# Two weight loads asked for by another engine, and four gates computed in one go, in a fused attention and mixture-of-experts kernel

## The chip, the cores and the metric

The kernel runs on one core of a Trainium2 chip. The time is device microseconds from launch to end, lower is better, given as the median of several executions. The profile shows one more execution, in which every instruction was recorded; its "span" runs from the first instruction to the last.

A core has five engines that run side by side, each through its own list of instructions in order: PE (TensorE, matrix products), DVE (VectorE), ACT (ScalarE), POOL (GpSimd) and SP (SyncE, which here only asks for transfers). Transfers between the main memory and the on-chip memory (DMAs) are asked for by SP, ACT or POOL, each through a queue of its own, and carried out by 16 DMA engines[...]. [...]

## What is computed

```python
def reference(**kwargs):
    attn_out = _attn_ref(q, k, v)            # softmax attention inside chunks of 64 tokens
    x = attn_out.transpose(0, 2, 1, 3).reshape(B * S, H * D)      # 4608 tokens x 512
    return _moe_ref(x, expert_emb, tau, w1, w2)

def _moe_ref(x, expert_emb, tau, w1, w2):
    ...
    logits = xn @ en.T / tau                 # 8 experts
    expert_idx = np.argmax(logits, axis=1)
    probs = softmax(logits)
    gate_w = probs[np.arange(N), expert_idx]
    for e in range(E):
        mask = expert_idx == e
        h = np.maximum(x[mask] @ w1[e], 0.0)               # 512 -> 1024
        out[mask] = gate_w[mask, None] * (h @ w2[e])       # 1024 -> 512
    return out
```

All of it is in 32-bit floats. Each token goes to the one expert that fits it best, and its output is scaled by the gate, the softmax weight of that expert. Since the chosen expert has the largest logit, the gate is 1 / sum(exp((logit - max) / |x|)).

## The kernel before

**Two stages.** The first, some 170 us, computes attention for 36 blocks of 128 tokens, finds each token's expert, and writes each token's row (512 values, its 8 logits, its number and its sum of squares) with an indirect DMA from POOL into `spots`, a table in main memory that is sorted by expert. The second stage runs over *steps*. A step takes two groups of 64 tokens, one from each of two streams: stream s = 0 works upwards from expert 0, stream s = 1 downwards from expert 7. The first four steps (NE = 4) are sure to belong to experts 0 and 7; for the later ones DVE works out tables (`src_row`, `eblk`, `fresh`, `swap`, `after`, `more_e`) in `places` and `behind`, at the turn from the first stage to the second.

**What a step j does.** SP loads the tokens' rows with `load_x(j)`: for each stream two DMAs into `xin` (three buffers) and one small one into `spot`. DVE turns the rows (`turn_xb`) and adds up quarters of them (`add_x`). `gate_parts(j)` computes the gate: a square root on ACT, four small instructions on DVE, an exponential with a sum on ACT, two small instructions on DVE. It is a generator, so its caller places each piece among other work. `hidden_fast(j)` computes relu(x @ w1) by Strassen's scheme in Winograd's form: seven products p1, p2, p3, p5, p6, p7, p4, in this order, of quarters of x with quarters of w1 (B11, B12, B21, B22) and with their differences T1, T2, T3, T4. PE does the products (L337), ACT copies the first out of PSUM (the tile U) and applies the relu, DVE combines (L369). `result(j)` multiplies by w2 (64 records on L408), ACT scales with the gate into `y`, of which there is one buffer, and POOL writes the rows to the output by an indirect DMA (L427). In the loop, pass j does hidden_fast(j + 1) and then result(j).

**The differences of w1.** `add_up(s, ...)` has DVE compute T1 to T4, 128x1024 values each (L286). For the first experts, T1, T2 and T4 of stream 0 come in pass 0 and of stream 1 in pass 1; T3 replaces B12 itself, and so comes in pass 1 after step 2, which still uses plain products (`hidden_plain`). T3 is first used by p7 of hidden_fast(3).

**Weights.** w1 and w2 of one expert are 2 MB each, per stream, so a load of both streams is 4 MB. `w2_sb` has two buffers, alternating from step 5 on (LONE = 5): the steps 0 to 4 use buffer 0. `load_when` asks for a load under a condition that is read from a table: `fresh` is 0 where a buffer holds the right expert already, and then nothing moves, but PE's wait on the load still ends only when SP has come to it. For step 5 the condition always holds, as buffer 1 is empty. `next_w1` holds w1 of the expert to come; `load_behind(j)` asks for it under the condition `more_e`, which is always true for the first one, j = 3. `take_next(j)` takes it over at a change of expert: three copies on POOL and the differences on DVE. In the trace the first such copy is at 298 us.

**SP's order around the change.** SP works through its list strictly in order: load_x(4), load_x(5), load_w2(5); pass 1: load_x(6), load_behind(3); pass 2: load_x(7), load_behind(4); pass 3: load_x(8), load_w2(4), load_behind(5); pass 4: load_x(9), load_w2(6), and so on. The order was written by hand (`manual_schedule`); the waits between engines come from the tile framework. POOL's list there: the last rows and padding rows into `spots`, a memset of `pad_late`, then one output DMA per step, and the copies of take_next.

**Pads.** `pad` sets a few unused floats at the start of a memory pool, which shifts the addresses of what follows. The pools `keep` and `blk` lie below all others; `qk` (first stage) and `late` (second stage) begin at the same place above them.

Of the kernel before, what the change touches and what calls it, by code (L numbers as in the profile page):

```python
# [9 lines left out]
FP32 = mybir.dt.float32  # L10
BF16 = mybir.dt.bfloat16
I32 = mybir.dt.int32
AF = mybir.ActivationFunctionType
ALU = mybir.AluOpType
# [4 lines left out]
P = 128  # L19
# [6 lines left out]
def kernel(  # L26
# [36 lines left out]
    def buf_of(j):  # L63
        return 0 if j < LONE else (j - LONE + 1) % 2
# [66 lines left out]
    def number(ap, top, *engines):  # L131
        return nc.values_load(  # L132
            ap,
            engines=engines,
            min_val=0,
            max_val=top,
            skip_runtime_bounds_check_because="a count of comparisons, less than this",
        )
# [27 lines left out]
        r0 = (0, E - 1)[s] * R + G * j  # L166
        return spots[r0 : r0 + G * n, :]

    def load_when(w, rows, e, f):

        e, f = number(e, E - 1, ENG.SP), number(f, 1, ENG.SP)
        nc.sync.dma_start(
            out=whole(w), in_=rows[:, ds(e, 1), :], cond=f > 0, max_dma_last_dim=4096
        )

    def load_w2(j):
        for s in range(2):
            at = of_step(s, j)
            load_when(w2_sb[s][buf_of(j)], w2_rows, eblk[at], fresh[at])

    def load_behind(j):

        c = LEAST - 2 - j
        for s in range(2):
            at = (slice(G * s, G * s + 1), slice(c, c + 1))
            load_when(next_w1[s], w1_rows, after[at], more_e[at])

    def load_late(j):
        for s in range(2 if j != LEAST else 1):
# [21 lines left out]

    def gate_parts(j):
        lg = spot[:, j % SPOTS, 0:E]
        rn = bp.tile([P, 1], FP32, tag="rn", name="rn", bufs=4)
        lmax = bp.tile([P, 1], FP32, tag="lmax", name="lmax", bufs=4)
        sh = bp.tile([P, E], FP32, tag="sh", name="sh", bufs=4)
        last = "_last" if j == LEAST - 1 else ""
        gate = bp.tile([P, 1], FP32, tag="gate" + last, name="gate", bufs=5)
        nc.scalar.activation(rn, spot[:, j % SPOTS, SQ : SQ + 1], AF.Sqrt)  # L219
        yield  # L220
        nc.vector.tensor_reduce(lmax, lg, axis=AX.X, op=ALU.max)
        nc.vector.tensor_scalar(rn, rn, 1e-6, None, ALU.add)  # L222
        nc.vector.reciprocal(rn, rn)
        nc.vector.tensor_scalar(sh, lg, lmax, rn, ALU.subtract, ALU.mult)
        yield
        nc.scalar.activation(sh, sh, AF.Exp, accum_out=gate)  # L226
        yield
        nc.vector.tensor_scalar(gate, gate, 1e-9, None, ALU.add)
        nc.vector.reciprocal(gate, gate)
        gate_of[j] = gate  # L230

    def hidden_part(j, s, b, w1, pool, tag, ps=None):

# [211 lines left out]
    with (  # L445
# [13 lines left out]
        NX = 2 * RB  # L459
        xr = one.tile([P, NX, W], FP32, name="xr")  # L460
        blank = one.tile([P, W], FP32, name="blank")
        pad(qk_p, 40, "pad_qk")
        ident = one.tile([P, P], FP32, name="ident")
        make_identity(nc, ident)
        rl_ps = ps_l.tile([P, 4 * RB * E + 2 * P], FP32, name="rt_ps")
# [638 lines left out]
        places(0, 2)  # L1104
        turn_xb(2)
        early_parts(NT + 3, 0)
        first_gates = [gate_parts(j) for j in range(4)]
        for g in first_gates:
            next(g)
        places(2, NST)  # L1110
        nc.vector.tensor_copy(n_steps, mid[0:1])
        nc.vector.tensor_copy(n_odd, odd[0:1])
        behind()

    late_p = ctx.enter_context(tc.tile_pool(name="late", bufs=1, reuse_waits="tile"))
    pad(late_p, 40, "pad_late")
    for s in range(2):
        w2_sb[s].append(late_p.tile([P, KF, D], FP32, name=f"w2_{s}1"))

# [2 lines left out]

    load_x(NE)
    load_x(NE + 1)
    load_w2(LONE)

    with (
        tc.tile_pool(name="ps_h", bufs=1, space=PSUM, reuse_waits="tile") as ps_h,
        tc.tile_pool(name="ps_y", bufs=2, space=PSUM, reuse_waits="tile") as ps_y,
    ):  # L1130
        H_PS = [P, G // Q, KF * Q]

        def hidden_plain(j, w1, behind_it=None):
            for s in range(2 if j != LEAST else 1):
                ps = bank(ps_h, H_PS)
                for b in range(G // Q):
                    hidden_part(j, s, b, w1, None, None, ps)
                if behind_it is not None:
                    behind_it(s)

        def first_parts():
            for g in first_gates:
                next(g, None)

        first_parts()
        for j in range(LEAST - 1):
            n = j + 2

            def turn_next():
                if n < LEAST:  # L1150
                    turn_xb(n)
                    if n + XBUF < NJ:
                        load_x(n + XBUF)
                    add_x(n)

            def swap_next():
                if NE <= n < LEAST:
                    take_next(n)

            if j == 0:  # L1160
                first_parts()
                add_up(0, None, TS)
                first_parts()
            elif j == 1:
                turn_next()
                add_up(1, None, TS)
                hidden_plain(2, w1_sb, lambda s: add_up(s, None, ("T3",)))
            else:
                gate = gate_parts(n) if n < LEAST else iter(())
                hidden_fast(j + 1, ps_h, gate, turn_next, swap_next)  # L1170

            result(j, ps_y)
            if NE <= next_of(j) < NJ:
                load_w2(next_of(j))
            if NE - 1 <= n < LEAST - 1:
                load_behind(n)
            elif n == LEAST - 1:
                load_late(LEAST)

        steps = number(n_steps, NST, ENG.PE, ENG.DVE, ENG.Activation, ENG.Pool, ENG.SP)  # L1180

        odd_one = number(n_odd, 1, ENG.PE, ENG.DVE, ENG.Activation, ENG.Pool, ENG.SP)

        def before_last():
            result(LEAST - 1, ps_y)
            load_w2(LEAST + 1)

        def step_alone(j, between=None):
            turn_xb(j)
            if j + XBUF < NJ:  # L1190
                load_x(j + XBUF)
            gates(j)
            hidden_plain(j, next_w1)
            if j + 1 < NJ:
                load_late(j + 1)
            if between is not None:
                between()
            result(j, ps_y)
            if j + 2 < NJ:
                load_w2(j + 2)  # L1200

        def more(j):
            if j == NJ:
                return

            with tc.If(steps > j - NE - 1):  # L1206
                step_alone(j)
                more(j + 1)

        had, had_mo, had_gate = dict(xin), dict(mo), dict(gate_of)  # L1210
        with tc.If(odd_one > 0) as if_odd:  # L1211
            step_alone(LEAST, before_last)
            more(LEAST + 1)
        for now, then in ((xin, had), (mo, had_mo), (gate_of, had_gate)):
            now.clear()
            now.update(then)
        with if_odd.Else():
            del xin[LEAST]
            load_x(LEAST + XBUF)
            before_last()  # L1220
            load_w2(LEAST + 2)
            load_late(LEAST + 1)
            more(LEAST + 1)
# [28 lines left out]
```

## Time and profile before

| | |
|---|---|
| median of 3 runs | 657.39 us (654.38 to 658.06) |
| the profiled execution | 657.75 us, span 656.0 us |
| PE busy | 617.0 us, 94% of the span |
| ACT busy | 429.7 us, 66% |
| DVE busy | 425.3 us, 65% |
| POOL busy | 183.9 us, 28% |
| DMA queue q1 (SP's): moved, share of the 16 engines' span | 71.99 MB, 34.0% |
| DMA queue q0 (POOL's) | 38.89 MB, 17.5% |
| PE's granted clock, mean | 0.993 |

A line of the timeline has the start in us, the length in us, the engine, the line of the code, the operation, its output and inputs, and the number of instructions merged into it; in brackets stands how long the engine sat idle before it and what ended that. "SPq" is SP's queue: what is listed there is the issue of a DMA, not its transfer. A line of waits has the waiting instruction, what it waited for, and then the total in us, how often, and the longest.

### The profile page before, as it was taken

The page shows a single profiled execution, that of the slowest core. Times are in us where ns is not written, and L with a number is a line of the kernel's source. Part 1 is how long each engine was busy: PE and PEld are TensorE (multiplying, and loading weights), DVE is VectorE, ACT ScalarE, POOL GpSimd, SP SyncE. Part 2 cuts the span into 40 slices and gives each one's busy share as a digit, 9 for nine tenths or more (in the row PEclk, how much of TensorE's full clock was granted, in tenths as well). Part 3 has the DMA queues.
Part 4 walks back from the last instruction along what each step waited for, and adds up shares of the span by engine and source line. Part 5 has one row for each costly group of instructions (what it writes and reads, how often), then busy time and mean ns, then how long its engine had stood idle before and what let it go on. Part 6 is the DMA issues. An engine that isn't in the chain of part 4 may idle for free. (4 is left out here: it accounts for less than half of the span.)

```text
span 656.0 us, 24867 instructions
## 1 busy us (share of the span) xinstructions
PE 617.0 (94%) x9744; PEld 344.5 (53%) x9744; DVE 425.3 (65%) x1140; ACT 429.7 (66%) x758; POOL 183.9 (28%) x262
## 2 busy tenths in 40 slices
PE   6899989898898989999999999999999999999993
PEld 5778878775443435445444544665444444444431
DVE  4878888786697446647784566979546666654430
ACT  4767767674316757767676767776777777676650
POOL 7759897762410100003020002303010021000101
PEclk9999999999998999999999999999999999999998
DMA  9999999988528711112787111776821116311111
GB/s 259 302 253 276 275 293 283 333 280 299 220 64 304 285 41 40 46 39 72 285 316 265 53 44 43 292 302 236 341 62 44 47 39 217 129 39 35 51 32 36
DMA packets 91696, 112.68 MB, mean 172 GB/s; under 512 B 49260, under 2 KB 69484, under 8 KB 91560
## 3 DMA queue, kind: packets, MB, share of 16 engines
q1 hardware_dynamic: 79512, 71.99, 34.0%
q0 software_dynamic: 12016, 38.89, 17.5%
q8 instruction: 81, 1.33, 0.8%
q14 instruction: 55, 0.45, 0.2%
q10 hardware_dynamic: 32, 0.02, 0.0%
HBM read 334.71 MB, written 22.69 MB: 545 GB/s over the span
## 5 line engine op out<-in xcount | busy, mean ns | idle before, releaser
L408 PE MATMUL y_ps<-w,hT 128*32 128x512 f32 (+1 forms) x2368 | 278.0, 587 | 2.9 <-DMA w<-in_moe_w_dram 2.9
L356 ACT ACTIVATE h<-C 64x256 f32<-64x256 f32 x264 | 179.4, 679 | 69.9 <-DVE C L369 67.1
L408 PEld LDWEIGHTS y_ps<-w,hT 128*32 128x32 f32 x2368 | 91.2, 110 | 155.4 <-issue 136.0
L427 POOL DMA_INDIRECT out_dram<-y,spot x36 | 37.5, 1042 | 392.4 <-ACT y L420 301.6
L337 PE MATMUL h<-w,S 128*32 128x256 f32 x1056 | 108.4, 382 | 1.8 <-DVE w L286 1.8
L337 PE MATMUL h<-sums,xbT 128*32 128x256 f32 x1056 | 109.0, 383 | 0.5 <-DVEq L294 0.5
L369 DVE TENSOR_TENSOR C<-C,h 128x256 f32<-128x256 f32 x231 | 96.0, 416 | 11.2 <-PE h L337 4.4
L363 DVE STREAM_TRANSPOSE hT<-h 128x512 f32<-128x512 f32 x66 | 46.7, 708 | 55.2 <-ACT h L356 54.5
L337 PE MATMUL h<-w,xbT 128*32 128x256 f32 x1056 | 82.3, 379 | 0.0
L222 DVE TENSOR_SCALAR rn<-rn 128x1 f32<-128x1 f32 x37 | 5.6, 151 | 87.6 <-ACT rn L219 87.6
L337 PEld LDWEIGHTS h<-w,S 128*32 128x32 f32 x1056 | 49.3, 110 | 24.2 <-DVE w L286 1.5
L337 PEld LDWEIGHTS h<-sums,xbT 128*32 128x32 f32 x1056 | 49.4, 111 | 23.2 <-DVEq L294 1.4
L337 PEld LDWEIGHTS h<-w,xbT 128*32 128x32 f32 x1056 | 43.6, 110 | 31.6 <-issue 9.0
L420 ACT ACTIVATE y<-y_ps,gate 128x512 f32<-128x512 f32 x36 | 24.8, 688 | 50.6 <-issue 44.7
L337 PE MATMUL h<-sums,S 128*32 128x256 f32 x528 | 53.4, 379 | 0.0
L816 POOL DMA_INDIRECT spots<-xr,dest x36 | 37.4, 1039 | 28.0 <-DVE dest L781 9.8
L198 DVE STREAM_TRANSPOSE xbT<-xin 128x256 f32<-128x256 f32 x73 | 44.4, 646 | 0.5 <-DVE hT L363 0.5
L219 ACT ACT_TABLE_LOAD x34 | 43.6, 1283 | 0.9 <-issue 0.4
L226 ACT ACT_TABLE_LOAD x34 | 43.6, 1283 | 0.6
L698 ACT COPY xT<-tr 128x512 f32<-128x512 f32 x36 | 21.1, 586 | 32.3 <-PE tr L696 32.3
L586 POOL DMA_DIRECT2D kx<-in_k_dram x36 | 31.9, 888 | 13.4 <-PE tr L612 12.6
L586 POOL DMA_DIRECT2D qx<-in_q_dram x40 | 34.5, 865 | 0.7 <-PE tr L612 0.6
(204 smaller groups left out, 802.2 us busy)
## 6 DMA issues: line engine op xcount, KB each, us to landing
w<-in_moe_w_dram SPq DMA_DIRECT2D x74, 2048.0 KB
next_w<-in_moe_w_dram SPq DMA_DIRECT2D x67, 2048.0 KB
xin<-spots SPq DMA_DIRECT2D x158, 64.0 KB
qx<-in_q_dram POOLq DMA_DIRECT2D x32, 256.0 KB, 5.9
v<-in_v_dram SPq DMA_DIRECT2D x58, 128.0 KB
kx<-in_k_dram POOLq DMA_DIRECT2D x28, 256.0 KB, 4.6
spots<-blank SPq DMA_DIRECT2D x9, 144.0 KB
spot<-spots SPq DMA_DIRECT2D x80, 4.0 KB
```

The costliest lines, as they stand in the source:

```text
L198: nc.vector.transpose(xT[:, :, cols].rearrange("p c (b i) -> p b c i", i=Q), t[:, s * (D // 2) : (s + 1) * (D // 2)].rearrange("p (b i c) ...
L219: nc.scalar.activation(rn, spot[:, j % SPOTS, SQ : SQ + 1], AF.Sqrt)
L226: nc.scalar.activation(sh, sh, AF.Exp, accum_out=gate)
L337: nc.tensor.matmul(ps[t0 : t0 + Q], lhsT=a[:, c, s], rhs=w[:, r], start=c == 0, stop=c == KD // 2 - 1,)
L356: nc.scalar.activation(h[b][G * v : G * v + G, s].rearrange("p (k i) -> p k i", i=Q), x[G * s : G * s + G].rearrange("p (i k) -> p k i", i=Q),
L363: nc.vector.transpose(hT.rearrange("p k (s b i) -> p b s k i", b=2, i=Q)[:, b], h[b].rearrange("p s (k i) -> p s k i", i=Q),)
L369: nc.vector.tensor_tensor(out, a, b, op)
L408: nc.tensor.matmul(ps[Q * r : Q * r + Q, 0:w], lhsT=d["hT"][:, c, Q * t0 : Q * t0 + Q], rhs=w2_sb[s][buf_of(j)][:, c, d0 : d0 + w], start= ...
L420: nc.scalar.activation(y[:, 0:w], ps[:, 0:w], AF.Copy, scale=gate_of.pop(j))
L427: ins = nc.gpsimd.indirect_dma_start(out=to, out_offset=bass.IndirectOffsetOnAxis(ap=at, axis=0), in_=y[:, 0:w], in_offset=None, bounds_ch ...
L586: eng.dma_start(out=x[done : done + n], in_=src[b, :, s : s + n, :].rearrange("h p d -> p h d"),)
L816: ins = nc.gpsimd.indirect_dma_start(out=spots, out_offset=bass.IndirectOffsetOnAxis(ap=at, axis=0), in_=m, in_offset=None, bounds_check=S ...
```

## The change

The change has three parts. The load of w2 for step 5 and the first load of the next w1 (load_behind(3)) are asked for by POOL instead of SP; both keep their place in the code, and thus come on POOL's list after the memset of pad_late and after the output DMA of step 1. The gates of steps 0 to 3 are computed by one set of instructions on tiles of four columns; the sum of the exponentials becomes a reduction on DVE. Some small tiles get two buffers instead of four, and two pads are 32 floats instead of 40.

```diff
-    def load_when(w, rows, e, f):
-        e, f = number(e, E - 1, ENG.SP), number(f, 1, ENG.SP)
-        nc.sync.dma_start(
+    def load_when(w, rows, e, f, by=(nc.sync, ENG.SP)):
+        e, f = number(e, E - 1, by[1]), number(f, 1, by[1])
+        by[0].dma_start(
             out=whole(w), in_=rows[:, ds(e, 1), :], cond=f > 0, max_dma_last_dim=4096
         )
+    BY_POOL = (nc.gpsimd, ENG.Pool)
-    def load_w2(j):
+    def load_w2(j, *by):
...
-    def load_behind(j):
+    def load_behind(j, *by):
...
     def gate_parts(j):
-        rn = bp.tile([P, 1], FP32, tag="rn", name="rn", bufs=4)
-        lmax = bp.tile([P, 1], FP32, tag="lmax", name="lmax", bufs=4)
-        sh = bp.tile([P, E], FP32, tag="sh", name="sh", bufs=4)
+        rn = bp.tile([P, 1], FP32, tag="rn", name="rn", bufs=2)
+        lmax = bp.tile([P, 1], FP32, tag="lmax", name="lmax", bufs=2)
+        sh = bp.tile([P, E], FP32, tag="sh", name="sh", bufs=2)
...
+    def first_gate_parts():
+        lg, sq = spot[:, 0:NE, 0:E], spot[:, 0:NE, SQ]
+        rn = bp.tile([P, NE], FP32, name="rn4", bufs=1)
+        lmax = bp.tile([P, NE], FP32, name="lmax4", bufs=1)
+        sh = bp.tile([P, NE, E], FP32, name="sh4", bufs=1)
+        gate = bp.tile([P, NE], FP32, name="gate4", bufs=1)
+        nc.scalar.activation(rn, sq, AF.Sqrt)
+        yield
+        nc.vector.tensor_reduce(lmax, lg, axis=AX.X, op=ALU.max)
+        nc.vector.tensor_scalar(rn, rn, 1e-6, None, ALU.add)
+        nc.vector.reciprocal(rn, rn)
+        for by, op in ((lmax, ALU.subtract), (rn, ALU.mult)):
+            nc.vector.tensor_tensor(sh, lg, by.unsqueeze(2).to_broadcast([P, NE, E]), op)
+            lg = sh
+        yield
+        nc.scalar.activation(sh, sh, AF.Exp)
+        yield
+        nc.vector.tensor_reduce(gate, sh, axis=AX.X, op=ALU.add)
+        nc.vector.tensor_scalar(gate, gate, 1e-9, None, ALU.add)
+        nc.vector.reciprocal(gate, gate)
+        for j in range(NE):
+            gate_of[j] = gate[:, j : j + 1]
...
-        pad(qk_p, 40, "pad_qk")
+        pad(qk_p, 32, "pad_qk")
...
-        first_gates = [gate_parts(j) for j in range(4)]
-        for g in first_gates:
-            next(g)
+        first_gates = first_gate_parts()
+        next(first_gates)
...
-    pad(late_p, 40, "pad_late")
+    pad(late_p, 32, "pad_late")
...
-    load_w2(LONE)
+    load_w2(LONE, BY_POOL)
...
-        first_parts()
+        next(first_gates)
         for j in range(LEAST - 1):
...
             if j == 0:
-                first_parts()
+                next(first_gates)
                 add_up(0, None, TS)
-                first_parts()
+                next(first_gates, None)
...
             if NE - 1 <= n < LEAST - 1:
-                load_behind(n)
+                load_behind(n, *([BY_POOL] if n == NE - 1 else []))
```

## The prediction

> **What bounds the kernel now.** I read the page's busy table first, then who TensorE waited for, then the timeline around those waits. PE is busy 617.0 of 656.0 us. From 175 us on it is the bound: its result() blocks repeat every 12.92 us (last three lines of the PE fence below: 236.02, 248.96, 261.87) and it hardly stops. So this change can only win where PE stops between 178 and 240 us, the steps it touches.
>
> PE's waits between 178 and 240 us (total, times, longest): there are two reasons only, one for each half of the change.
> ```profile
> PE y_ps L408 <- DMA w<-in_moe_w_dram: 2.9, 2, 2.6
> PE h L337 <- DVE w L286: 1.8, 2, 1.0
> ```
> PE's timeline (start, length): products of hidden_fast(3), then result() of steps 4, 5 and 6.
> ```profile
> 199.16 1.05 PE L337 MATMUL h<-sums,S 128*32 128x256 f32 x16
> 201.00 0.63 PE L337 MATMUL h<-w,S 128*32 128x256 f32 x4 [0.80 <-DVE w L286]
> 202.66 1.44 PE L337 MATMUL h<-w,S 128*32 128x256 f32 x10 [1.03 <-DVE w L286]
> ...
> 234.71 1.05 PE L408 MATMUL y_ps<-w,hT 128*32 128x512 f32 x4 [2.63 <-DMA w<-in_moe_w_dram]
> ...
> 236.02 6.63 PE L408 MATMUL y_ps<-w,hT 128*32 128x512 f32 x58 [0.26 <-DMA w<-in_moe_w_dram]
> ...
> 248.96 6.61 PE L408 MATMUL y_ps<-w,hT 128*32 128x512 f32 x58
> 261.87 6.61 PE L408 MATMUL y_ps<-w,hT 128*32 128x512 f32 x58
> ```
> *Stop A* (200.2 to 202.7): product p7 wants T3 of both streams from DVE. DVE's timeline shows why T3 is late: it works without a gap from 185.5 on, and the gates stand in front.
> ```profile
> 185.59 0.15 DVE L221 TENSOR_REDUCE lmax<-spot 128x1 f32<-128x8 f32 x1
> ...
> 188.19 1.22 DVE L286 TENSOR_TENSOR sums<-w 128x1024 f32<-128x1024 f32 x1
> ...
> 191.84 0.15 DVE L228 TENSOR_SCALAR gate<-gate 128x1 f32<-128x1 f32 x1
> ...
> 192.88 1.23 DVE L198 STREAM_TRANSPOSE xbT<-xin 128x256 f32<-128x256 f32 x2
> ...
> 199.67 1.18 DVE L286 TENSOR_TENSOR w<-w 128x1024 f32<-128x1024 f32 x1
> ...
> 201.40 1.21 DVE L286 TENSOR_TENSOR w<-w 128x1024 f32<-128x1024 f32 x1
> ```
> *Stop B* (232.1 to 236.0): result(4) wants load_w2(4), whose transfer is not even wanted (the same expert, so its condition is false; nothing moves from 236 to 238 us): PE goes on 0.1 us after SP *issues* it at 234.60. SP is late because its earlier issues stood behind weights:
> ```profile
> 194.97 2.03 SPq L172 DMA_DIRECT2D w<-in_moe_w_dram  x2
> 198.24 1.43 SPq L148 DMA_DIRECT2D xin<-spots  x2
> 199.87 4.88 SPq L154 DMA_DIRECT2D spot<-spots  x1
> ...
> 210.43 1.94 SPq L172 DMA_DIRECT2D next_w<-in_moe_w_dram  x2
> ...
> 215.22 5.20 SPq L154 DMA_DIRECT2D spot<-spots  x1
> ...
> 234.60 1.40 SPq L172 DMA_DIRECT2D w<-in_moe_w_dram  x2
> ```
> A spot issue costs 0.51 us on an unloaded queue (190.68, 192.94); behind 4 MB of w2 or w1 it costs 4.88, 2.30 (at 206.62), 5.20 and 1.96 (at 222.18). SP's own list for a step takes about 11.5 us of the 12.9, so it makes up hardly 1.4 us per step.
>
> [...]the granted clock is 0.50 from 202.8 to 206.1. It was not halved at stop B, though 2.63 us of it are wholly idle[...]. [...] SP's w2 load moved at about 360 GB/s (195 to 208 us, with 0.5 MB of rows beside it).
>
> **The change part by part.**
>
> *Gates at once.* Removed from DVE ahead of T3: four chains of four instructions, 185.59 to 188.19 = 2.60 us, and four pairs, 191.84 to 192.88 = 1.04 us. Added: one max-reduce, two small operations, two tensor_tensor of 32 columns; later one sum-reduce and two small ones. Nearest rows: a 128x4 from 128x32 reduce is 176 ns (L740), a 128x32 tensor_tensor 192 ns (L741); dependent ones follow 0.22 us apart in pick(). With the old pitches for the small ones (0.07, 0.18, 0.20) the first part takes 0.07+0.18+0.20+0.22+0.23 = 0.90 and the second 0.22+0.18+0.20 = 0.60. Saved 1.70+0.44 = 2.14 us (bounds 1.8 and 2.4 for 0.2 either way). ACT loses three Sqrts, three Exps and four accumulator reads; it waited 7.3 us for sh there, so nothing. The x and hT turned between have landed or been computed early, so DVE stays packed and T3 moves as a whole: stream 0 from 200.85 to 198.71, stream 1 from 202.61 to 200.47. PE is free for p7 at 200.21, does stream 0's four records in 0.22, and meets stream 1 at 200.52 instead of 202.66: 2.14. The idling is then about 0.1 us, so the half clock goes too: 3.3 us at half speed, 1.65. **A = 3.8 us.** If the clock were halved all the same, 2.1.
>
> *w2 of step 5 by POOL.* POOL is free from 181.28 (its pad_late memset) and its table values exist since 177.9, so after about 1.5 us of reading registers (SP's gap, 193.45 to 194.97) it issues at 182.8 to 185 instead of SP's 195 to 197. Behind it on POOL: out(0), which waits for ACT's y until about 191; its issue is not delayed. POOL's issue of 256 KB takes 0.87 us (L586); I take 1 us for each 2 MB, bounds 0.5 and 3. result(5) wants it at 249: no gain in itself. The load needs about 13 us at before's rate, so it ends at 196 to 197; out(0) stands behind it in the queue and lands by 198. y has one buffer: ACT's y(1), at 200.38 now and 198.24 after, waits for out(0). PE feels that only when the U copy behind y(1) holds up p4's bank, at about 201.05, so there are 1.9 us of slack from 198.24. Cost 0.
>
> *w1 by POOL.* It is issued behind out(1), at about 201 instead of 210.4, and lands by 214; it is first used at 298. out(2), due about 211, lands at 214, before y(3) at about 222. The new wait: SP's load_behind(4) writes the same buffer and so waits for this landing, to 214. Behind it on SP stand load_x(8) and load_w2(4).
>
> *SP afterwards.* load_x(4) and (5) as now to 193.4 (up to 3 more while POOL's load fills the engines), load_x(6) 195 to 199.5, load_x(7) from 202.9 (DVE's turn of x(4)) to 207.4, load_behind(4) 214 to 215.4, load_x(8) 216.6 to 221.1, load_w2(4) from 222.6, or 222.2 if PE's result(3) were later. PE wants it at 231.65 - 3.8 = 227.8. Slack 4 us, so stop B goes wholly: 232.08 to 236.02 is 3.94, less 0.43 for four records' own work. **B = 3.5 us.** Nothing else is late next: the following load_w2(6) has until about 253.
>
> *Pads and buffer counts.* 32 bytes more in blk, 32 less in the two pads above it; rn, lmax and sh are used once per step, so two buffers do. 0.
>
> Sum 7.3 us. Against the rhythm: from result(1) (188.84) to result(2) (206.01 less 0.22) is 16.95, so 4.0 over 12.92; from result(3) (219.01) to result(4) (236.02 less 0.43) is 16.58, so 3.7 over. The ceiling is 7.7. After 240 us everything runs on PE and moves as one. The profiled execution took 657.75 (span 656.0 and 1.75 around it), the median is 657.39; the sum gives 650.4 and 650.1. With the ceiling 649.7: **650.0 us**.
>
> **Rivals.** *Only A*: the SP part stays because load_behind(4) waits for w1 beyond 218 us or load_x is slowed by POOL's traffic. For: the new wait is real. Against: 4 us of slack. 657.4 - 3.8 = 653.6. *Only B*: DVE's chain does not shorten, since something else holds T1 or the turn. Against: DVE's only wait there is 0.2 us. 653.9.
> *Given back*: out(0) lands at about 203, y(1) and p4 are 3 us late and the clock halves again; A is eaten, then a part of B: 655 to 659.
> *Slower*: GpSimd's queue moves such loads slowly. At 200 GB/s w2 ends at 204, out(0) at 205, PE loses 4.9 at p4 and 1.65 of clock; w1, issued at 207, lands at 228 and load_w2(4) comes at 238 where PE wants it at 234: 3.7. Together 10.2 against 7.5 won: 660. It decides below about 215 GB/s. For: no 4 MB on that queue in the trace, and y has one buffer. Against: [...]259 to 333 GB/s over both queues in the first 160 us.
>
> **How the numbers follow.** Forecast 0.70 (its own range 648.5 to 651.5), only A 0.09, only B 0.04, given back 0.09, slower 0.08. The range 648.3 to 654.2 holds the first three. About 0.5%, 3.3 us, can be told from no change; 653.6 and 653.9 lie just beyond 654.1, so I count four fifths of them: faster 0.80, within 0.12, slower 0.08.
>
> **What would show it.** Right: no half clock near 203; p7's second part within 0.3 us of p6's end; no PE wait on w in result(4); spot issues near 0.5 us at 195 to 225; w2's landing before y(1). Wrong: ACT's y(1) waiting on a DMA, SP waiting for next_w far past 218, or POOL stuck for several us in a weight issue.

## The result, and the profile after

| | before | after |
|---|---|---|
| median, same chip, 17 executions each | 657.67 us (652.68 to 661.41) | 651.28 us (647.94 to 656.44) |
| ratio after / before, 95% interval | | 0.9911 [0.989, 0.9933] |
| the profiled execution | 657.75 us, span 656.0 | 649.77 us, span 648.1 |
| PE's granted clock, mean | 0.993 | 0.994 |

The change makes the kernel 0.9% faster; 0.0089 of 657.67 is 5.85 us (the two medians differ by 6.39), where 7.3 was the sum predicted. The time lies in the predicted range, and near the upper end of the forecast's own (648.5 to 651.5). All ratios here compare the faster executions of each kernel and leave out those that are over 1.5% above its fastest, so they need not be the quotient of the medians beside them.

The two spans differ by 7.9 us, more than the ratio says, so they have to be cut up. I cut where PE begins result(0) and result(6): between these PE is the bound, and the change lies there. PE's timelines have the start of result(0), in the kernel before (first line) and after (second):
```profile
175.06 3.19 PE L408 MATMUL y_ps<-w,hT 128*32 128x512 f32 x28
...
171.30 4.90 PE L435 MATMUL y_ps<-w,hT 128*32 128x512 f32 x44
```

| | before | after | difference |
|---|---|---|---|
| start of the span to result(0) | 175.06 us | 171.30 us | -3.76 |
| *the stretch*: result(0) to result(6) | 85.98 us | 80.37 us | -5.61 |
| result(6) to the end of the span | 394.9 us | 396.4 us | +1.5 |

The first row is the attention stage, which the change leaves alone. Over six profiles of this kernel, of its parts and of the kernel before, taken where the kernel before needs 656 to 658 us, result(0) starts anywhere from 171.28 to 176.89 us, and the kernel before has 171.28 in one and 175.06 in another. That row is within the scatter, and so is the third: from result(6) on, the fourteen profiles of this document take 393.5 to 397.3 us. The stretch is the change's own: 5.61 us, near the 5.85 of the ratio. From here on times are told relative to the start of result(0), which takes the scatter out.

The stretch has six gaps. If PE never stopped it would take 13.78 + 5 x 12.91 = 78.33 us (the shortest seen of each gap in before and after):

| gap, us | 0 to 1 | 1 to 2 | 2 to 3 | 3 to 4 | 4 to 5 | 5 to 6 | sum |
|---|---|---|---|---|---|---|---|
| before | 13.78 | 16.35 | 13.40 | 16.12 | 13.42 | 12.91 | 85.98 |
| after | 13.78 | 12.91 | 12.91 | 14.48 | 13.38 | 12.91 | 80.37 |

Stop A (gaps 1 to 3) is gone whole: 3.93 us. Of stop B (gaps 3 to 5) only 1.68 us are gone, and 2.0 are left.

PE's timeline of the kernel after (start, length, instructions merged, idle time before in brackets) shows both. The first two lines are p6 and p7 of hidden_fast(3), the last two are result(4):
```profile
195.40 1.05 PE L364 MATMUL h<-sums,S 128*32 128x256 f32 x16
196.26 1.11 PE L364 MATMUL h<-w,S 128*32 128x256 f32 x14
...
225.38 1.05 PE L435 MATMUL y_ps<-w,hT 128*32 128x512 f32 x4 [1.12 <-DMA w<-in_moe_w_dram]
...
226.65 6.63 PE L435 MATMUL y_ps<-w,hT 128*32 128x512 f32 x58 [0.22 <-DMA w<-in_moe_w_dram]
```
p7 follows p6 with no bracket, in one piece, with the granted clock at 1.00 from 195.94 to 199.35 us: before, it came in two pieces behind 0.80 and 1.03 us of idling, and the clock was 0.50 behind them. result(4) still stops, for 1.12 + 0.22 us instead of 2.63 + 0.26.

DVE's timeline of the kernel after, the lines that answer to those of before:
```profile
181.86 0.19 DVE L244 TENSOR_REDUCE lmax<-spot 128x4 f32<-128x32 f32 x1
...
182.56 1.22 DVE L313 TENSOR_TENSOR sums<-w 128x1024 f32<-128x1024 f32 x1
...
186.22 0.18 DVE L253 TENSOR_REDUCE gate<-sh 128x4 f32<-128x32 f32 x1
...
186.74 1.22 DVE L201 STREAM_TRANSPOSE xbT<-xin 128x256 f32<-128x256 f32 x2
...
193.52 1.18 DVE L313 TENSOR_TENSOR w<-w 128x1024 f32<-128x1024 f32 x1
...
195.25 1.22 DVE L313 TENSOR_TENSOR w<-w 128x1024 f32<-128x1024 f32 x1
```
The first gate part takes 182.56 - 181.86 = 0.70 us and the second 0.52, against 2.60 and 1.04: 2.42 us saved. T3 of stream 1 (last line) starts 195.25 - 171.30 = 23.95 after result(0), against 201.40 - 175.06 = 26.34: it moved by 2.39, all of it.

SP's issues (start, how long SP was held by the issue), first the beginning of load_x(4) in the kernel before, then the kernel after:
```profile
182.78 1.43 SPq L148 DMA_DIRECT2D xin<-spots  x2
...
179.04 1.43 SPq L148 DMA_DIRECT2D xin<-spots  x2
181.44 5.55 SPq L148 DMA_DIRECT2D xin<-spots  x2
187.51 1.94 SPq L154 DMA_DIRECT2D spot<-spots  x1
...
199.57 5.15 SPq L148 DMA_DIRECT2D xin<-spots  x2
204.91 4.34 SPq L154 DMA_DIRECT2D spot<-spots  x1
...
214.59 0.51 SPq L154 DMA_DIRECT2D spot<-spots  x1
216.67 1.46 SPq L172 DMA_DIRECT2D next_w<-in_moe_w_dram  x2
...
225.27 1.35 SPq L172 DMA_DIRECT2D w<-in_moe_w_dram  x2
```
The last line is load_w2(4), and PE goes on 0.11 us behind it (225.38), as it did before: stop B has the same cause as before, SP's being late. It comes 53.97 us after result(0), instead of 59.54: SP gained 5.57 us. It starts the list as it did before, 7.74 us after result(0) (179.04 - 171.30) against 7.72 (182.78 - 175.06). Yet SP no longer issues the two large loads, and its row loads are still held: 5.55 and 1.94 us at load_x(4) (179.04 to 187.51), 5.15 and 4.34 us at load_x(6) (199.57 and 204.91). The first pair of load_x(4), at 179.04, still went at the usual price; the hold begins with the second.

Who holds them is seen on POOL's timeline of the kernel after:
```profile
177.44 0.82 POOL L172 DMA_DIRECT2D w<-in_moe_w_dram  x1
178.53 0.80 POOL L172 DMA_DIRECT2D w<-in_moe_w_dram  x1 [0.28 <-PE y_ps L435]
...
187.88 1.06 POOL L454 DMA_INDIRECT out_dram<-y,spot  x1 [8.54 <-ACT y L447]
...
196.82 0.81 POOL L172 DMA_DIRECT2D next_w<-in_moe_w_dram  x1 [0.58 <-DMA spot<-spots]
198.88 0.79 POOL L172 DMA_DIRECT2D next_w<-in_moe_w_dram  x1 [1.25 <-DMA xin<-spots]
```
POOL asks for w2 at 177.44, and load_x(4) runs into that transfer. It asks for w1 at 196.82, and load_x(6) runs into that one. The windows of the kernel after (span; busy time of PE, PEld, DVE, ACT and POOL with the number of instructions; PE's clock; DMA share; GB/s) say why:
```profile
180.00:185.00 5.00, 5.00 (x100) 3.02 (x96) 4.69 (x20) 0.23 (x1) 0.00 (x0) 1.00 1.00 394
...
200.00:210.00 10.00, 10.00 (x144) 7.13 (x140) 5.85 (x18) 8.39 (x14) 1.04 (x1) 1.00 1.03 406
```
All 16 DMA engines are full (share 1.00 and 1.03) at 394 and 406 GB/s, all queues together, while SP is held. With the weights on SP's own queue, in the kernel before, it was much the same: 1.02 at 416 GB/s from 199.35 to 202.76 us. And the hold has hardly changed: the row loads load_x(4) to load_x(8) take 34.9 us of SP's time in the kernel before and 36.0 in the kernel after. What SP has gained is the price of the issues it no longer makes.

From the page of the kernel after, the DMA queues (packets, MB, share of 16 engines) and POOL's issues of w2 (KB each, median us from issue to landing):
```profile
q1 hardware_dynamic: 77400, 63.60, 30.9%
q0 software_dynamic: 14128, 47.28, 21.0%
...
w<-in_moe_w_dram POOLq DMA_DIRECT2D x2, 2048.0 KB, 13.7
```
POOL's queue carries 47.28 - 38.89 = 8.39 MB more and SP's as much less: the two loads of 4 MB. The last line is the w2 load: 13.7 us from issue to landing, near the 13 predicted.

### The profile page after: what moved, and what is told of

Its sections match the earlier page's. It is cut to its first block, busy times and chain, and to the rows that moved or that the text cites. A ratio compares the mean times of both kernels' runs of the same rounds, so it can differ in the third digit from the quotient of the medians.

```text
span 648.1 us, 24845 instructions
## 1 busy us (share of the span) xinstructions
PE 615.0 (95%) x9744; PEld 350.5 (54%) x9744; DVE 423.6 (65%) x1124; ACT 428.6 (66%) x748; POOL 188.0 (29%) x266
## 3 DMA queue, kind: packets, MB, share of 16 engines
q0 software_dynamic: 14128, 47.28, 21.0%
## 5 line engine op out<-in xcount | busy, mean ns | idle before, releaser
L435 PEld LDWEIGHTS y_ps<-w,hT 128*32 128x32 f32 x2368 | 93.7, 110 | 150.6 <-issue 132.0
L364 PE MATMUL h<-sums,xbT 128*32 128x256 f32 x1056 | 107.0, 379 | 0.6 <-DVEq L321 0.6
L364 PE MATMUL h<-w,S 128*32 128x256 f32 x1056 | 106.7, 379 | 0.0
L390 DVE STREAM_TRANSPOSE hT<-h 128x512 f32<-128x512 f32 x66 | 46.7, 708 | 55.2 <-ACT h L383 54.5
L447 ACT ACTIVATE y<-y_ps,gate 128x512 f32<-128x512 f32 x36 | 24.8, 688 | 48.4 <-issue 43.0
## 6 DMA issues: line engine op xcount, KB each, us to landing
w<-in_moe_w_dram POOLq DMA_DIRECT2D x2, 2048.0 KB, 13.7
```

What stands on the lines that cost most here:

```text
L364: nc.tensor.matmul(ps[t0 : t0 + Q], lhsT=a[:, c, s], rhs=w[:, r], start=c == 0, stop=c == KD // 2 - 1,)
L390: nc.vector.transpose(hT.rearrange("p k (s b i) -> p b s k i", b=2, i=Q)[:, b], h[b].rearrange("p s (k i) -> p s k i", i=Q),)
L435: nc.tensor.matmul(ps[Q * r : Q * r + Q, 0:w], lhsT=d["hT"][:, c, Q * t0 : Q * t0 + Q], rhs=w2_sb[s][buf_of(j)][:, c, d0 : d0 + w], start= ...
L447: nc.scalar.activation(y[:, 0:w], ps[:, 0:w], AF.Copy, scale=gate_of.pop(j))
```

## Experiments

**The theories.** *The parts add*: stops A and B are two losses, each removed by its own half of the change (the prediction's sum). *SP keeps its own time*: from result(0) to load_w2(4) SP works through its list at a pace that hardly depends on PE, and PE can't pass result(4) before SP gets there. Then the gates alone gain nothing, since stop B grows by what stop A loses, and the gain of the whole is SP's advance. On what holds SP: *the engines are full*, so that its rows wait for weights whoever asked for them, against *its own queue was full of weights*, so that moving them to POOL frees it.

The kernels ran in three sets, each on one chip. In the second set the kernel before takes 656.36 us there, as in the measurement above. In the first and third it takes 668.97 and 669.43 us, and that turned out to matter. (The chips are recorded as number 10, 15 and 15; whether the second and the third are the same one is not known.)

| set, run | before | this | ratio [95%] | result(0) at | stretch | load_w2(4) issued after result(0) |
|---|---|---|---|---|---|---|
| 1 gates_only | 668.97 | 669.31 | 0.9999 [0.9979, 1.002] | 195.43 | 79.84 | 53.4 |
| 1 loads_only | 668.97 | 669.15 | 0.9997 [0.9974, 1.002] | 189.53 | 80.04 | 48.4 |
| 1 w2_4_by_pool | 668.97 | 671.09 | 1.0036 [1.0016, 1.0056] | 194.56 | 78.34 | by POOL |
| 1 w1_later | 668.97 | 667.30 | 0.9984 [0.9956, 1.0012] | 191.66 | 78.34 | 46.7 |
| 2 before_again | 656.36 | 654.29 | one execution | 171.28 | 86.80 | 59.01 |
| 2 after_again | 656.36 | 650.07 | 0.9884 [0.982, 0.9947] | 174.19 | 80.38 | 53.99 |
| 2 gates_only_2 | 656.36 | 658.41 | 1.0024 [0.9995, 1.0052] | 176.89 | 87.25 | 59.72 |
| 2 loads_only_2 | 656.36 | 652.32 | 0.9942 [0.9901, 0.9984] | 173.93 | 82.68 | 56.28 |
| 3 w2_4_by_pool_2 | 669.43 | 671.13 | 1.0037 [1.0018, 1.0057] | 193.59 | 80.12 | by POOL, 50.8 |
| 3 w1_later_2 | 669.43 | 669.16 | 0.9959 [0.9926, 0.9993] | 192.59 | 80.60 | 48.95 |
| 3 small_pieces | 669.43 | 677.32 | 1.0125 [1.0061, 1.0189] | 194.87 | 89.21 | 62.3 |
| 3 after_third | 669.43 | 668.64 | 1.0007 [0.9979, 1.0036] | 191.90 | 80.36 | 49.16 |

Times are in us; the three columns on the right come from the profile of each run.

### First set: the halves, and two ways to take load off SP

**gates_only** is the kernel after, its pads and buffer counts too, with both loads asked for by SP again.
```diff
-    load_w2(LONE, BY_POOL)
+    load_w2(LONE)
...
-                load_behind(n, *([BY_POOL] if n == NE - 1 else []))
+                load_behind(n)
```


> The changed kernel with both weight loads given back to SP, so only the gates of the first four steps are computed at once. Measure: from the start of result(0) to the start of result(6) on PE, 85.98 us before, 80.37 after, 78.33 if PE never stopped. Theory 'SP keeps its own time': SP's list from load_x(4) to load_w2(4) does not wait for PE, so load_w2(4) is still issued 59.5 us after the start of result(0); stop A goes (no wait on T3, no half clock), but stop B grows by what A gave, to some 7 us, and the stretch stays at 85.5 to 86: no gain in time. Rival, as in the prediction's 'only A': the two stops add up, the stretch is 82.0 and the time 3.8 us below before.

**loads_only** is the kernel before, with both loads asked for by POOL.
```diff
-    load_w2(LONE)
+    load_w2(LONE, BY_POOL)
...
-                load_behind(n)
+                load_behind(n, *([BY_POOL] if n == NE - 1 else []))
```


> The kernel before with only the two loads given to POOL; gates step by step as before. Theory 'SP keeps its own time': load_w2(4) is issued about 54 us after the start of result(0), as in the changed kernel, and PE, held up by stop A, wants it only at 56.5: stop B is gone wholly, stop A stays with its half clock, the stretch from result(0) to result(6) is 82.3 and the time 3.7 us below before. Rival (the two parts add, B being worth 1.5 us as seen in the changed kernel): stretch 84.4, time 1.5 below before.

**w2_4_by_pool** is the kernel after, with load_w2(4) too asked for by POOL, so that SP's list can't hold result(4).
```diff
-                load_w2(next_of(j))
+                load_w2(next_of(j), *([BY_POOL] if j == NE - 1 else []))
```


> The changed kernel, with load_w2(4), whose condition is false, also asked for by POOL, behind the output DMA of step 3. Theory: what is left of stop B (1.6 us) is only SP coming late to this one issue; POOL comes to it at about 51 us after the start of result(0), before PE's 52.5, so the stretch is 78.3 to 78.6 and the time 1.5 to 2.1 below the changed kernel, about 649.4. Rival: POOL comes later than SP since it waits for ACT's y(3): the stretch grows above 80.4.

**w1_later** is the kernel after, with the load of w1 asked for at pass 4 instead of pass 1, away from load_x(6).
```diff
-                load_behind(n, *([BY_POOL] if n == NE - 1 else []))
+                if n > NE - 1:
+                    load_behind(n)
+                if n == 6:
+                    load_behind(NE - 1, BY_POOL)
```


> The changed kernel with the first load of the next w1 asked for by POOL in pass 4 instead of pass 1 (it is used 40 us after that). Theory 'the 16 engines are full': SP's issues of rows are slow wherever 4 MB of weights are under way, on whichever queue; without w1 there, load_x(6) takes SP 4.5 us instead of 12.1, load_w2(4) comes about 8 us earlier, stop B is gone, the stretch is 78.3 to 78.6. Rival 'SP's own list is simply too long': load_x(6) still takes over 8 us, the stretch stays near 80.4.

Measured: neither half does anything, 0.9999 and 0.9997, and w1_later's 0.9984 can't be told from 1. No theory expected that. The profiles differ from the first pair at once, before the change is reached: result(0) starts at 189.5 to 195.4 us instead of 171 to 177, and the stretch is 78.3 to 80.0 us in all four. Two kernels have the 78.33 of a PE that never stops, so there was no stop left to win here. So I took the halves again, beside unaltered kernels.

### Second set: the same halves where the stops are there

**before_again** and **after_again** are the two kernels as they are; **gates_only_2** and **loads_only_2** are those above.

> The kernel before once more, for its trace beside the next three on one chip. Theory 'a late PE hides both stops': where the first four experiments ran, PE reached result(0) only at 190 to 195 us, held up by the issue of its own instructions, while DVE's and SP's lists ran on; if that holds here, the kernel before too has a stretch from result(0) to result(6) of 78.5 to 81 us instead of 85.98, and there is little to win. Rival: before keeps its stretch of about 86 here too, and what the changed kernels win in it they lose in the first stage, by 6 us.

> The changed kernel once more. Where result(0) comes at about 171 to 175 us: a stretch of 80 to 81 and about 0.991 of before. Where it comes at 190 us or later: a stretch of 78.3 to 79.5, and 0.997 to 1.000 of before.

> Only the gates at once; both weight loads asked for by SP. Where result(0) comes at 171 to 175 us, 'SP keeps its own time' expects load_w2(4) about 59.5 us after the start of result(0) and a stretch of 85.5 to 86, no gain; the rival (the stops add up) a stretch of 82.0 and 3.8 us won. Where result(0) comes late, both expect a stretch of 79 to 81.

> Only the two loads given to POOL, gates step by step. Where result(0) comes at 171 to 175 us, 'SP keeps its own time' expects stop A with its half clock to stay and stop B to be gone: a stretch of 82.3, 3.7 us won; the rival (B worth 1.5) 84.4. Where result(0) comes late, a stretch of 79 to 81.

Measured: the change's gain came again, 0.9884 [0.982, 0.9947]. Gates alone gain nothing (1.0024), nor do the pads and buffer counts that come with them; loads alone gain 0.58% (0.0058 x 656.36 = 3.8 us). The intervals of the loads alone and of the whole change overlap; what tells these two apart is the stretch, 82.68 and 80.38, in one profile each. The gaps, from result to result:

| gap, us | 0 to 1 | 1 to 2 | 2 to 3 | 3 to 4 | 4 to 5 | 5 to 6 | sum |
|---|---|---|---|---|---|---|---|
| before_again | 13.77 | 15.16 | 12.91 | 17.28 | 14.77 | 12.91 | 86.80 |
| gates_only_2 | 13.77 | 12.91 | 12.91 | 20.24 | 14.51 | 12.91 | 87.25 |
| loads_only_2 | 13.77 | 16.09 | 13.72 | 12.91 | 13.28 | 12.91 | 82.68 |

In gates_only_2 stop A is gone (12.91 and 12.91), and what it left has been added to stop B (20.24). PE's waits from 178 to 245 us in gates_only_2 (waiting line, reason, total, times, longest), the only line in that view:
```profile
PE y_ps L435 <- DMA w<-in_moe_w_dram: 6.9, 1, 6.9
```
SP's timeline of gates_only_2, the issue of load_w2(4):
```profile
236.61 1.40 SPq L172 DMA_DIRECT2D w<-in_moe_w_dram  x2
```
PE's timeline of gates_only_2, its answer:
```profile
236.72 3.71 PE L435 MATMUL y_ps<-w,hT 128*32 128x512 f32 x14 [6.88 <-DMA w<-in_moe_w_dram]
```
PE reaches result(4) early and stands for 6.88 us until SP issues load_w2(4), 236.61 - 176.89 = 59.72 us after result(0). In before and before_again that was 59.54 and 59.01. With the loads on its own queue, SP's pace doesn't know of the gates: this is *SP keeps its own time*, and it takes the prediction's rival "only A, 653.6 us" away. The parts don't add.

loads_only_2 is the other half. PE's waits from 178 to 245 us in loads_only_2:
```profile
PE h L340 <- DVE w L289: 1.9, 2, 1.0
```
SP's timeline of loads_only_2, the issue of load_w2(4):
```profile
230.21 1.35 SPq L172 DMA_DIRECT2D w<-in_moe_w_dram  x2
```
PE's timeline of loads_only_2, result(4) behind it:
```profile
230.42 0.60 PE L411 MATMUL y_ps<-w,hT 128*32 128x512 f32 x2
```
Stop A is there as before (1.9 us in two waits), and at the start of result(4) there is no bracket: PE comes late enough for SP, at 56.28. With A's delay back, stop B is hidden but for 0.37 us in the gap behind it, and the stretch is 82.68, 4.1 less than before_again's. SP was expected at 54, so with the loads on POOL its pace is not quite its own: POOL asks for w1 behind the output of step 1, which here comes 27.94 us after result(0) instead of 25.52 in the kernel after, and the transfer runs into load_x(7) (held for 5.84 and 5.13 us) instead of load_x(6).

before_again answers a question that the first profile had raised. PE's timeline of before_again at stop A and at stop B:
```profile
197.22 0.63 PE L337 MATMUL h<-w,S 128*32 128x256 f32 x4 [0.80 <-DVE w L286]
198.88 0.84 PE L337 MATMUL h<-w,S 128*32 128x256 f32 x10 [1.04 <-DVE w L286]
...
230.40 4.10 PE L408 MATMUL y_ps<-w,hT 128*32 128x512 f32 x16 [3.78 <-DMA w<-in_moe_w_dram]
```
The same idling of 0.80 and 1.04 us was not followed by half clock at stop A here (1.00 from 196 to 204 us), and the gap was 15.16 instead of 16.35. Stop B was longer (3.78 us of idling instead of 2.63 + 0.26), and there the clock was 0.50 behind it (231.05 to 234.47 us). PE began result(4) at about the same place, 59.12 us after result(0) (230.40 - 171.28) against 59.65 (234.71 - 175.06), and the stretch came to 86 to 87 us both times. The half clock at A had cost nothing that the wait for SP would not have taken.

At A the clock was 0.50 once and 1.00 the other time; the traces show how the idling lay. In the twelve of the fourteen that have more than one spell of half clock, the spells start a whole number of steps of 3.413 us apart (in the kernel before at 202.76 and 649.91 us, 131 steps), and each lasts one step or two, 3.41 or 6.83 us, but for the last, at the end of the span. Windows cut at these steps, first one of the kernel before, then two of before_again (columns as above):
```profile
199.35:202.76 3.41, 1.58 (x24) 0.53 (x20) 3.33 (x5) 2.89 (x6) 0.97 (x1) 1.00 1.02 416
...
196.92:200.33 3.41, 2.08 (x32) 1.11 (x36) 3.13 (x9) 3.36 (x5) 0.97 (x1) 1.00 1.04 420
...
231.05:234.47 3.42, 3.42 (x18) 0.79 (x20) 0.76 (x2) 1.17 (x2) 0.00 (x0) 0.50 0.00 0
```
In the kernel before both idle pieces fall into one step (PE busy for 1.58 of 3.41 us), and the step behind it has half clock. In before_again a step ends at 196.92, within the first piece; the step of the second has PE busy for 2.08 us, and the clock stays at 1.00. Stop B there idles 2.76 us of one step, and the next, the last line, has 0.50. Stop B of the kernel before is spread over two steps (230.07 to 233.48 and 233.48 to 236.89 us), with PE busy for 2.02 and 1.92 us, and the clock stays at 1.00. These are the cases looked at; what decides it was not shown.

### Third set: what holds SP

> The changed kernel with load_w2(4) also asked for by POOL. Where result(0) comes at 171 to 177 us: stop B, 1.3 us of waiting and 2.0 us in the stretch, is gone, since POOL is at this load about 51 us after the start of result(0); stretch 78.3 to 78.6 against 80.4, time 0.988 of before. Rival: POOL is held by its output DMA of step 3 and comes later than SP's 54: stretch above 80.4. Where result(0) comes late, the stretch is 78.3 and nothing is won.

> The changed kernel with the first load of the next w1 asked for by POOL in pass 4 instead of pass 1. Where result(0) comes at 171 to 177 us: 'the engines are full' expects load_x(6) to take SP 4.5 us instead of 12, load_w2(4) 46 to 47 us after the start of result(0) instead of 54 (or as soon as PE has done with result(3), 46.5), a stretch of 78.3 to 78.6. Rival 'SP's list is too long': load_x(6) over 8 us, stretch near 80.4.

**small_pieces** is the kernel after, with POOL's two loads asked for in runs of at most 256 numbers (1 KB) instead of 4096.
```diff
-            out=whole(w), in_=rows[:, ds(e, 1), :], cond=f > 0, max_dma_last_dim=4096
+            out=whole(w), in_=rows[:, ds(e, 1), :], cond=f > 0,
+            max_dma_last_dim=4096 if by[1] == ENG.SP else 256,
```


> The changed kernel with POOL's two weight loads cut into pieces of 1 KB instead of 4 KB or more. Open is why SP's row loads are slow to issue beside weights on another queue. 'Turns by packets': if a DMA engine finishes a run of large pieces of POOL's queue before it takes one of SP's, smaller pieces shorten SP's waits: the second pair of xin issues of load_x(4), 5.6 us before, takes under 3, load_w2(4) comes 50 us or less after the start of result(0), stretch 78.3 to 78.6. 'Share of bytes': if SP only gets too little of full engines, the pieces change nothing: 5 to 6 us again, or longer for the cost of more pieces, stretch 80.4 or more.

> The changed kernel unaltered, as the measure for the other three on this chip: stretch 80.4, about 0.990 of before where result(0) comes at 171 to 177 us; 78.3 to 79.5 and 0.997 to 1.000 where it comes at 190.

after_third, unaltered, gains nothing in this set (1.0007), like the halves of the first. Its profile says where the difference lies. PE's timeline of after_third, around the start of result(0):
```profile
191.88 0.45 PE L275 MATMUL h_ps<-w,xbT 128*32 128x256 f32 x1 [0.89 <-issue]
...
193.32 5.13 PE L435 MATMUL y_ps<-w,hT 128*32 128x512 f32 x36 [0.48 <-issue]
```
The windows of after_third around it (columns as above):
```profile
188.00:192.00 4.00, 2.32 (x11) 0.67 (x11) 2.29 (x12) 0.00 (x0) 3.08 (x4) 1.00 0.09 25
...
192.06:195.47 3.41, 2.93 (x15) 0.94 (x16) 1.13 (x3) 1.84 (x3) 1.99 (x4) 0.50 0.44 95
```
SP's timeline of after_third:
```profile
194.05 1.56 SPq L148 DMA_DIRECT2D xin<-spots  x2
196.58 6.46 SPq L148 DMA_DIRECT2D xin<-spots  x2
...
223.55 5.98 SPq L154 DMA_DIRECT2D spot<-spots  x1
...
241.06 1.60 SPq L172 DMA_DIRECT2D w<-in_moe_w_dram  x2
```
PE crawls through the plain products ahead of result(0), 11 records in 4 us, for a reason the profile calls "issue": it shows no engine and no transfer that PE waits for (DMA share 0.09). From the start of the last 64 of these products to result(0) it takes 8.96 us (182.94 to 191.90), where the kernel after takes 3.48 (167.82 to 171.30). The other 15 us by which after_third is late have gathered before, and there DVE and SP are late with PE. Over the crawl SP doesn't wait. It begins load_x(4) 194.05 - 191.90 = 2.15 us after result(0), where in after it was 7.74 and in before 7.72. This parts all fourteen profiles: 7.71 to 7.74 us in the six of the second set and the first pair, 1.80 to 2.33 in the eight of the first and third sets. With these 5.6 us of start SP is at load_w2(4) 49.16 us after result(0), before PE wants it (52.5 if nothing stops: 13.78 + 3 x 12.91), and there is no stop B: every gap of after_third but the first is 12.91. The first is 15.81, as half clock follows the crawl (the line at 192.06). So its stretch of 80.36 is that of the kernel after by chance. Half clock in the first gap also makes the 80.60 and 80.12 us of w1_later_2 and w2_4_by_pool_2: result(0) begins there with 17 records in 4.46 us and 12 in 3.12, where the kernel after has 44 in 4.90. The two of 78.34 are at the 78.33 of a PE that never stops. Neither half of the change is needed in these sets. loads_only, with the old gates, has no stop A (12.91 and 12.91). In gates_only SP issues everything itself and comes at 53.4, and the gaps around result(4) lose 0.85 us. So the kernel before should hardly stop there either, and its equal time fits; it was not profiled there.

SP's timeline of w1_later_2 at load_x(7), whose spot issue in after_third is held for 5.98 us (the line at 223.55):
```profile
222.76 1.31 SPq L148 DMA_DIRECT2D xin<-spots  x2
224.26 0.51 SPq L154 DMA_DIRECT2D spot<-spots  x1
...
262.18 5.69 SPq L148 DMA_DIRECT2D xin<-spots  x2
```
Without a load of w1 under way the same issue takes 0.51 us. Here POOL asks for w1 at 257.90 and 259.82, and now it is the pair at 262.18 that is held (the last line), as is one in w1_later (5.76 us). The hold has moved with the load. Nothing of SP's own has changed between the two kernels, only what POOL had asked for. That is *the engines are full*. Its time, 0.9959 [0.9926, 0.9993], overlaps with that of after_third, the medians in the table hardly differ, and w1_later gave 0.9984: whether it beats the change isn't settled, and where stop B exists it was not tried.

w2_4_by_pool_2 does what was meant. POOL's timeline of that kernel:
```profile
243.25 1.03 POOL L454 DMA_INDIRECT out_dram<-y,spot  x1 [11.86 <-ACT y L447]
244.42 0.06 POOL L172 DMA_DIRECT2D w<-in_moe_w_dram  x1
```
POOL comes to load_w2(4) right behind out(3), 244.42 - 193.59 = 50.8 us after result(0). But there was no stop to remove in this set, and it costs 0.37% (0.36% in the first). Why is not explained by its stretch (78.34 and 80.12). Behind result(6) its two profiles take 397.3 and 396.2 us, against 393.5 to 395.5 in the other six of these sets, but the kernel after alone has 394.0 to 396.4 in three profiles. Where stop B exists it was not tried.

small_pieces was to settle in what way full engines are shared. SP's rows were held for less: its second pair of load_x(4) took 3.22 us, against 5.01 to 6.46 in the other three of this set. But POOL was held. POOL's timeline of small_pieces:
```profile
193.94 2.85 POOL L172 DMA_DIRECT2D w<-in_moe_w_dram  x1
...
206.60 2.80 POOL L172 DMA_DIRECT2D w<-in_moe_w_dram  x1 [9.81 <-issue]
...
237.01 2.79 POOL L172 DMA_DIRECT2D next_w<-in_moe_w_dram  x1 [11.16 <-DMA spot<-spots]
```
PE's waits from 165 to 300 us in small_pieces:
```profile
PE h L365 <- POOLq L322: 6.5, 1, 6.5
```
In the small pieces an issue takes 2.85 us instead of 0.8, and the second of a pair comes only 9.81 and 11.16 us after the first has ended. PE then waited 6.5 us for POOL, the stretch is 89.21, the time 1.0125. This is the "POOL stuck in a weight issue" that the prediction named as a danger: in the small pieces it came, and in the change's large ones each issue took 0.79 to 0.82 us. As only half of the load was under way when SP was held (POOL asked for the second 2 MB at 206.60), the shorter hold of SP proves nothing, and the way of sharing stays open.

## Why the prediction was right, and where its sum was not

- **Stop A, 3.8 us: right, 3.93 by the gaps.** DVE saved 2.42 (predicted 2.14, upper bound 2.4): both parts were each shorter than estimated, 0.70 and 0.52 against 0.90 and 0.60. T3 moved as a whole, p7 runs through, and the clock stays at 1.00.
- **POOL's loads: right.** 0.82 and 0.80 us for each 2 MB (1 taken), begun at 177.44 right behind the memset (the 1.5 us of reading registers that were taken do not show), 13.7 us to landing, which is before ACT's y(1) at 194.24. out(0) at 187.88 was held by ACT's y alone. The "slower" rival needed less than 215 GB/s; 394 and 406 were moved over all queues. (Of the rates that the prediction reads from the first 160 us, the lowest is 253 GB/s, not 259, which changes nothing.)
- **The new wait of load_behind(4) on w1's landing: harmless, as said.** It is issued at 216.67, 1.6 us after the issue before it has ended (214.59 + 0.51), which is about what load_w2(4) takes, 1.5 us (223.27 + 0.51 to 225.27); in both gaps the program reads two table values.
- **Stop B, 3.5 us: mis-sized, 1.68.** The step that failed is "SP afterwards". Load_x(4), which takes 4.8 us in the kernel before, was to take up to 3 us more, and load_x(6) 4.5 us, "195 to 199.5". From the first issue to the end of the last they took 10.4 (179.04 to 189.45) and 12.1 us (197.17 to 209.25). Load_w2(4) was to be at 222.6, 47.5 after result(0), with 4 us of slack; it came at 54.0, 6.4 later, and PE wanted it at about 52.5. So "stop B goes wholly" failed by 1.34 us of waiting and the restart around it. I had put SP's held issues down to weights on its own queue, and expected only "up to 3" from another's. SP saved just the issuing: 2.03 and 1.94 us for the pairs (in before) and the 1.5 us before each (193.45 to 194.97 and 208.92 to 210.43), in which the program reads two table values, 7.0 in all; of these the row loads took back 1.1 and the gaps between them 0.3. Two of the signs that the prediction named for being right therefore did not come: spot issues near 0.5 us (4.34 was seen at load_x(6)), and no wait on w in result(4).
- **The 1.65 us of half clock within A** went as said, but were not a gain by themselves: before_again had clock 1.00 at A and its stretch was no shorter (86.80 against 85.98).
- **The sum of A and B: a ceiling, not two gains.** With both stops gone the stretch would lose 85.98 - 78.33 = 7.65 us, as the prediction's rhythm has it. But the halves do not add: the stop that PE makes first delays it to where the later one is shorter. Measured where both stops exist: gates alone 0 us, loads alone 3.8, both 5.9 and 7.6 (0.9911 of 657.67 and 0.9884 of 656.36, with the intervals given). The gain of 5.6 in the profiles is SP's advance, 59.54 to 53.97, and A's part is that it lets PE use it. Of the rivals, "only B, 653.9" was nearly what loads_only_2 did, for the reason given; "only A, 653.6" was wrong on its own terms, since taking A away alone moves the wait and gains nothing.
- **The ceiling 7.7 and the range** held because the two errors were small beside what PE could win: A's gain was too small by 0.1, B's too large by 1.8. That the stops were there to be won at all in the measured pair was not in the prediction's hands: in two of three later sets the same change, or its parts, won nothing. So far the right number was luck.

SP was held for 5.01 to 6.46 us in one pair of row issues beside weights on POOL's queue, and its advance of 5.6 us is what is left of the 7.0 us of issues and table reads it no longer has. Its two issues, 2.03 and 1.94 us, are small beside the 13.7 us of one transfer, but in a list of some 11.5 us per step of 12.9 they and the reads ahead of them are the whole gain.

**Left open.** Why PE issues so slowly ahead of result(0) in two of the three sets, and what the other 15 us of lateness there are: neither a wait nor a transfer in the trace explains it, and whether it belongs to a chip was not tried. What w2_4_by_pool's 0.37% are. How engines that are full share between queues, and whether it is the engines or the memory behind them that sets their pace.

## What to carry to other kernels

Where two engines each work through a fixed list and meet at several waits, don't add up the stops: follow each list by itself from a common start, and take the later at each meeting; shortening one list gains only until the other is late. Moving the two 4 MB loads to POOL's queue took 7.0 us out of SP's list, but not the hold of the row loads beside them: five steps' rows took 34.9 us of SP's time before and 36.0 after, with the DMA share at 1.02 (199.35 to 202.76 us) before, and at 1.00 and 1.03 after. And a gain that hangs on who arrives first at a turn holds only where that order holds: here it was 0.9 to 1.2% where PE began result(0) 7.7 us ahead of SP's first row load, and nothing where it began 2 us ahead.

## What the runs showed of the hardware that was not expected

- While POOL's 4 MB load was under way (DMA share 1.00 from 180 to 185 us in the kernel after), the second pair of row loads of load_x(4), two of 64 KB, took SP 5.55 us to issue there, and 5.01 to 6.46 us in the other runs in which POOL asked for the load in large pieces. The first pair beside that load took 1.43 to 1.56 us, little more than the 1.3 to 1.4 with no load under way: not every issue was slow, the hold began with the second pair.
- The same two idle pieces of PE (0.80 and 1.03 or 1.04 us) were followed by clock 0.50 in the profile of the kernel before and by 1.00 in that of before_again. The two spells in the kernel before start 131 steps of 3.413 us apart (202.76 and 649.91 us). With both pieces in one step PE was busy for 1.58 us of it, and the next step had 0.50; with the first cut by the end of a step the later one had PE busy for 2.08 us, and the clock stayed at 1.00.
- In after_third PE spent 4 us on 11 records with the DMA share at 0.09, and the profile puts its waits down to "issue". SP began load_x(4) 2.15 us after result(0) there instead of 7.74, and a step with clock 0.50 followed (192.06 to 195.47 us).
- On POOL's queue a 2 MB load in pieces of 1 KB took 2.79 to 2.86 us to issue in small_pieces, and the second of a pair came 9.81 and 11.16 us after the first had ended; in the pieces of the change it took 0.79 to 0.82 us in the kernel after, and the second came after 0.28 and 1.25 us.
